# Seven x blocks instead of six, two weight tiles instead of three, and a new order inside a slot of an attention and ffn kernel

## The chip, the cores and the metric

The kernel runs on one core of a Trainium2 chip. The metric is device time in microseconds (us), the median of several runs of the same kernel. The core has five engines that work side by side, each through its own instructions in order: TensorE (PE in the profile, its weight loads PEld), VectorE (DVE), ScalarE (ACT), GpSimd (POOL), and SyncE (SP), which here issues nearly all DMA transfers.

## The reference

```python
def _attn_ref(q, k, v, tau):                      # batch 8, heads 8, sequence 576, head size 64
    scores = matmul(q, k.transpose(0, 1, 3, 2)) / sqrt(64)
    thresh = max(scores, axis=-1) - tau
    scores = where(scores >= thresh, scores, -1e9)
    attn = exp(scores - max(scores, axis=-1))
    attn = attn / (sum(attn, axis=-1) + 1e-09)
    return matmul(attn, v)

def _moe_ref(x, w_a, w_b, w_out):                 # x: 4608 x 512, w_a and w_b: 512 x 1536, w_out: 1536 x 512
    return (x @ w_a) * (x @ w_b) @ w_out
```

All is float32. The output of attention, with its eight heads put side by side, is the x of the second function ("ffn" below).

## The kernel before

**Units and slots.** Attention is cut into 160 units (i, u): i is one of 32 pairs of heads, u one of five query tiles (four of 128 rows, and a tail of 64 rows). The main loop runs over slots g = 0 to 162. Slot g starts unit g and does later steps of earlier units, so that several units are in flight. The order in which instructions are written in a slot is the order in which each engine runs them: `keep_order` fixes it at the end.

**What a slot holds.** From slot 9 on, the order in the program is:

- `scores` (L338): TensorE multiplies q and k of unit g into two PSUM tiles of two banks each (L350); VectorE takes the row maxima (two reductions, L357) and the threshold (L358).
- `turn_blocks` (L439) for unit g−1: VectorE transposes its weights in blocks of 32 (two L444, in place in the tile `tw`), and SP writes them to a scratch tensor in DRAM, `swap`, with four DMAs (L455).
- `advance` with 0.3 of the slot's pace: TensorE does so many columns of ffn work.
- `weigh` (L368) for unit g: ScalarE computes a bias (L377) and the exponential (L378) into a new `tw` tile; VectorE multiplies by the mask of the threshold and sums (L381).
- transposes of freshly loaded q and k (`prep`, L318).
- `advance` with 0.35 of the pace.
- in some slots `weighted` (L531): the product with v of a finished half of a pair (72 matmul records, L481), and the copies out of PSUM into an x block (`settle`, L488 on ScalarE and L490 on VectorE). It is preceded by `make_x`, see below.
- `turn_back` (L458) for unit g−2: SP reads `swap` back into a tile `wT` (one DMA of 576 KB, L464; two of 144 KB for a tail, L467). There are two `wT` tiles, so the DMA waits on SP's queue until the product that read the old content is through.
- `reciprocal` (L392, L394) and `normalise` (two L400 on ScalarE) for unit g.
- loads of q, k and v for later pairs, and stores of finished rows (SP).
- `advance` with 0.15 and 0.2 of the pace.

The first eight units take another way, with transposes on TensorE.

**ffn.** `ffn` (L651) is a generator; each step issues the matmuls of some columns. The products with w_a and w_b are partly plain (L686), partly in a form with seven products in the place of eight (`seven_of`, L587, matmuls in L624), and the product with w_out is L732 (also seven products, L778 for the first two blocks). A seven-product group of 64 matmul records is short, and six of seven groups need VectorE steps (L633 to L647).

**The pacing.** `advance(cols)` adds columns to `running["owed"]` and steps the generator until they are used up. The pace of a slot comes from the backlog and the slots until the next x block arrives; a product with v is deducted.

**x blocks.** Attention's output is gathered in tiles with tag `xT`, of which there are XT_BUFS. A block with the sums for the seven-product form takes four tiles while ffn reads it. `make_x` (L849), called before a product with v that opens a new x tile, counts the tiles in use and, while there are too many, forces ffn on:

```python
        while (len([k for k in x_of if k != (0, 0)]) + len(xtail_of) + len(complete) + sum(len(x) for x, _ in blocks)
               + (state["reading"] and running["tiles"]) + count > XT_BUFS):
            owed = running["owed"]
            running["owed"] = 0.0
            advance(1)
            running["owed"] += owed - 1
            store(len(pending))
```

The forced columns stay in `owed` as debt. A tile for the tails of four batches is in use for most of a half of the run.

**PSUM.** All matmul results go through one pool of four tiles (`banks`, L127), which are used in turn.

Of the kernel before, what the change touches and what calls it, by code (L numbers as in the profile page):

```python
# [21 lines left out]

PV_LAG = 3
BY_PE = 8
XT_BUFS = 6
H_BUFS = 3
Q_BUFS = 3
OSB_BUFS = 5
# [3 lines left out]
ROOM = 1024  # L32
PORTIONS = (0.3, 0.35, 0.15, 0.2)
RAWS = 3
TW_BUFS = 3
SEVENS = 2
BY_HEAD = 16

# [15 lines left out]
def kernel(  # L54
# [38 lines left out]
    nc = tc.nc  # L93
# [11 lines left out]
    R = 96  # L105
# [99 lines left out]
    sums_sb = sums_u32.bitcast(FP32)  # L205
# [71 lines left out]
    ROWS = 2 * NR * D  # L277
    rooms = []
    for _ in range(TW_BUFS):
        t = work.tile([P, 2 * NB, Q], FP32, tag="tw", bufs=TW_BUFS, name="rows")  # L280
        rooms.append(t.rearrange("p n e -> p (n e)")[0:R, 0:ROWS])
    rooms += [sums_sb[0:R, c:c + ROWS] for c in range(0, 5 * ROWS, ROWS)]
    rooms = [t.rearrange("p (n w) -> p n w", n=NR) for t in rooms]
    load_rows(0, "q", rooms[0])
    load_rows(0, "k", rooms[1], nc.scalar)
# [49 lines left out]
    def prep_copy(mT, tp):  # L335
        nc.vector.tensor_copy(mT.rearrange("p (c k) -> p c k", c=2), tp)

    def scores(i, u):  # L338
        qT, kT = prepared[i]["q" if i < HP else "q1" if u > 1 else "q0"], prepared[i]["k"]
        base = HALF if i >= HP and u > 1 else 0  # L340
        n = 2 if u < NT else 1
        sc = [banks(SH, "sc") for _ in range(n)]
        each = [(c, t, j) for c in range(2) for t in range(n) for j in range(2)]
        if units.index((i, u)) < BY_HEAD:
            each.sort(key=lambda x: x[2])
        for c, t, j in each:
            r = slice(j * D, (j + 1) * D)
            o = t if u < NT else 1 - j
            q0, to = (u * P + t * D if u < NT else MAIN) - base, slice(o * D, (o + 1) * D)
            nc.tensor.matmul(sc[j if u < NT else 0][to, c], qT[r, q0:q0 + D],  # L350
                             kT[r, c * SH:(c + 1) * SH], start=True, stop=True)
        mx = small.tile([P, 2], FP32, tag="mx", name="mx")
        thr = small.tile([P, 2], FP32, tag="thr", name="thr")
        bias = small.tile([P, 2], FP32, tag="bias", name="bias")
        for j in range(n):
            c = slice(j, j + 1)
            nc.vector.tensor_reduce(mx[:, c], sc[j], axis=AX.XY, op=ALU.max)  # L357
        nc.vector.tensor_scalar(thr[:, 0:n], mx[:, 0:n], cut, None, op0=ALU.subtract)  # L358
        scored[i, u] = (sc, thr, bias, mx)
# [79 lines left out]
    def turn_blocks(i, u):  # L439

        ws, _ = weights.pop((i, u))
        t = whole.pop((i, u))
        for w in ws:
            nc.vector.transpose(w, w)  # L444
        if u < NT:
            swap = scratch.tile([G, P, NSLOT * Q], FP32, tag="swap", name="swap")
        else:
            swap = scratch.tile([2, P, NSLOT * Q], FP32, tag="swapt", name="swap")
        swaps[i, u] = swap
        for g in range(G):  # L450
            if u < NT:
                to, n = swap[g], G
            else:
                to, n = swap[g % 2, (1 - g // 2) * D:(2 - g // 2) * D], 2
            nc.sync.dma_start(to.rearrange("(r p) e -> p r e", p=Q),  # L455
                              t[g * Q:(g + 1) * Q, 0:n * NSLOT].rearrange("p (r s) e -> p r (s e)", r=n))

    def turn_back(i, u):  # L458

        swap = swaps.pop((i, u)).rearrange("g p e -> p g e")  # L460
        if u < NT or i < HP:
            turned[i, u] = turned_tile()
            n = G if u < NT else 2
            nc.sync.dma_start(turned[i, u][:, 0:n].rearrange("p g s e -> p g (s e)"), swap)  # L464
        else:
            for y in range(2):
                nc.sync.dma_start(turned[i, 2 + y][:, G].rearrange("p s e -> p (s e)"), swap[:, y])  # L467
# [381 lines left out]
    def make_x(count):  # L849

        while (len([k for k in x_of if k != (0, 0)]) + len(xtail_of) + len(complete) + sum(len(x) for x, _ in blocks)
               + (state["reading"] and running["tiles"]) + count > XT_BUFS):
            owed = running["owed"]
            running["owed"] = 0.0
            advance(1)
            running["owed"] += owed - 1
            store(len(pending))

    def backlog():
# [29 lines left out]
    n = 0  # L889
# [4 lines left out]
    for g in range(len(units) + PV_LAG):  # L894
        written = len(pending)
        state["converted"] = state["added"]
        here = g < len(units)
        converting = bool(early.get(g)) or bool(early.get(g - 1))
        if here:
            i, u = units[g]  # L900
            scores(i, u)
        exchange_blocks()
        pace = (PACE if g > BY_PE else PACE_EARLY) * BLOCK_COLS
        if g > BY_PE:
            pace = min(pace, backlog() / (min([a for a in arrivals if a > g] + [len(units) + PV_LAG + 1]) - g))
        pace += NSLOT * S / 2 / (NT + 1) + CATCH_UP * max(backlog() - BLOCK_COLS, 0)
        if 2 <= g < BY_PE + 2:
            weighted_unit(*units[g - 2])
            running["owed"] -= NSLOT * P // 2
        if g < 3:  # L910
            prep_copy(*prep_pe(g + 1, "q"))
        convert_rest(g, 0)
        if g == 0:
            for c in range(0, 3 * QUARTER - 2 * CW + 1, 2 * CW):
                extra.append(more_u32[:, c:c + 2 * CW].rearrange("p (f w) -> p f w", w=2))
        if g == 3:
            for c in range(0, NSUM - 2 * CW + 1, 2 * CW):
                extra.append(sums_u32[:, c:c + 2 * CW].rearrange("p (f w) -> p f w", w=2))
        load_weights(RAWS)
        if g > BY_PE and g <= len(units):  # L920
            turn_blocks(*units[g - 1])
        if g > BY_PE:
            advance(PORTIONS[0] * pace)
        if here:
            weigh(i, u)
        if here and g < BY_PE:
            reciprocal(i, u, nc.vector)
        if 0 < g <= BY_PE:
            turn_pe(*units[g - 1])
        if g < 3:  # L930
            prep_copy(*prep_pe(g + 1, "k"))
        for p in range(HP, NPR):
            for name, d in (("q0", 2), ("k", 1), ("q1", 1)):
                if g == (second if name == "q1" else first)[p] - d:
                    prep(p, name)
        if g > BY_PE:
            advance(PORTIONS[1] * pace)
            n = g - PV_LAG
            if BY_PE <= n < len(units) and part(*units[n]):
                p, h = part(*units[n])  # L940
                if pairs[p][1] == 0:
                    make_x(2 if h == 1 and p >= HP and pairs[p][0] % GT == 0 else 1)
                make_room()
                weighted(*part(*units[n]))
                running["owed"] -= NSLOT * width(*part(*units[n])) // 2
            if BY_PE + 1 < g <= len(units) + 1:
                turn_back(*units[g - 2])
        for n in early.get(g, [])[:1]:
            convert_first(n)
            convert_clamp(n)  # L950
        if here and g < BY_PE:
            diagonals(i, u)
        elif here:
            reciprocal(i, u, nc.scalar if converting else nc.vector)
            normalise(i, u)
        convert_rest(g, 1)
        if g <= BY_PE:
            advance(pace)
        convert_rest(g, 2)
        for n in early.get(g, [])[1:]:  # L960
            convert_first(n)
            convert_clamp(n)
        load_weights(RAWS)
        for p in range(HP, NPR):
            for name, d in (("q0", 4), ("k", 3), ("q1", 3)):
                if g == (second if name == "q1" else first)[p] - d:
                    load(p, name)
        for p in range(1, NPR):
            if g == first[p] - 1:
                load_v(p)  # L970
        if BY_PE <= g < BY_PE + HP:
            load_v(g - BY_PE, again=True)
        store(written)
        if g > BY_PE:
            advance(PORTIONS[2] * pace)
            advance(PORTIONS[3] * pace)

        if not converting and not state["sums"]:
            state["slots"] = state.get("slots", 0) + 1
            for n in {1: (0,), 2: (1,), 3: (2,)}.get(state["slots"], ()):  # L980
                for z in range(2):
                    weight_sums(n, z)
            if state["slots"] >= 3 and state["through"]:
                for z in range(2):
                    weight_sums(3, z)
                state["sums"] = True
        if g > first[HP] + 1 and not converting and state["first"] < 3 * SEVENS:
            first_sums(state["first"] % 3, state["first"] // 3)
            state["first"] += 1
# [37 lines left out]
```

## Time and profile before

| what | value |
| --- | --- |
| median of 3 runs | 1502.7 us (1501.66 to 1507.4) |
| time of the profiled run | 1505.54 us |
| span of the profiled run, first to last instruction | 1503.7 us |
| mean granted TensorE clock | 0.984 |
| TensorE busy | 1401.6 us (93%) |
| VectorE busy | 1069.6 us (71%) |
| ScalarE busy | 687.7 us (46%) |
| GpSimd busy | 553.3 us (37%) |
| one L444 transpose, mean | 754 ns |
| one L357 maximum, mean | 749 ns |
| one L378 exponential, mean | 831 ns |
| one L381 thresholding, mean | 801 ns |
| one L400 normalisation, mean | 769 ns |

The page of a profile gives busy time per engine, the same in 40 slices of time with the granted TensorE clock, the DMA queues, the chain of work that ended last, and groups of instructions. In a group, "out<-in" names the tiles, then come the shapes, the count, the busy time, the mean of one, and the idle time of the engine just before them with what ended it. Other views answer questions on the same trace: waits (who waited for whom, total us, times, longest), stretches of time with each engine's busy time, and a timeline. The profiled run is the one whose span and durations are used; the median is of separate runs. Slot numbers are counted by the L350 matmuls, 16 records for a unit of 128 rows and 8 for a tail.

### The profile page before, as it was taken

The page shows a single profiled execution, that of the slowest core. Times are in us where ns is not written, and L with a number is a line of the kernel's source. Part 1 is how long each engine was busy: PE and PEld are TensorE (multiplying, and loading weights), DVE is VectorE, ACT ScalarE, POOL GpSimd, SP SyncE. Part 2 cuts the span into 40 slices and gives each one's busy share as a digit, 9 for nine tenths or more (in the row PEclk, how much of TensorE's full clock was granted, in tenths as well). Part 3 has the DMA queues.
Part 4 walks back from the last instruction along what each step waited for, and adds up shares of the span by engine and source line. Part 5 has one row for each costly group of instructions (what it writes and reads, how often), then busy time and mean ns, then how long its engine had stood idle before and what let it go on. Part 6 is the DMA issues. An engine that isn't in the chain of part 4 may idle for free.

```text
span 1503.7 us, 76562 instructions
## 1 busy us (share of the span) xinstructions
PE 1401.6 (93%) x34208; PEld 1231.2 (82%) x34208; DVE 1069.6 (71%) x2365; ACT 687.7 (46%) x1275; POOL 553.3 (37%) x724
## 2 busy tenths in 40 slices
PE   5789999999899999999997979899999999999998
PEld 4677687788899888889796878888789877888986
DVE  6798687888767786777647767667867877764434
ACT  5777355545454554544424435345444545431111
POOL 2664704433252525252623225251525161614100
PEclk9999999999999999999997999999999999999999
DMA  9976687668656775676526756367655776550000
GB/s 214 214 205 179 164 191 179 164 154 214 155 151 159 186 181 146 157 183 165 131 58 159 169 140 166 91 160 182 167 152 132 180 174 166 135 147 29 4 17 17
DMA packets 325081, 223.22 MB, mean 148 GB/s; under 512 B 169616, under 2 KB 308880, under 8 KB 324752
## 3 DMA queue, kind: packets, MB, share of 16 engines
q1 hardware_dynamic: 322384, 217.73, 59.0%
q8 instruction: 269, 4.41, 1.3%
q10 hardware_dynamic: 2368, 0.59, 0.2%
q14 instruction: 60, 0.49, 0.1%
HBM read 128.58 MB, written 89.65 MB: 145 GB/s over the span
## 4 chain that ended last, share of the span: by engine, by line
PE 77%; DVE 11%; DMA 4%; issue 3%; ACT 2%; SPq 2%; DVEq 0%; ACTq 0%
PE pab L624 20%; PE po L732 19%; PE pab L686 17%; PE pv L481 9%; PE sc L350 9%; DVE mx L357 3%; DMA wT<-swap 2%; DVE tw L444 2%; SPq L455 1%; DVE tw L381 1%; PE po L778 1%; DVE xT L490 1%; PE tp L425 1%; DVE low L258 0%; DMA qT<-in_q_dram 0%
## 5 line engine op out<-in xcount | busy, mean ns | idle before, releaser
L400 ACT ACTIVATE tw<-tw,rcp 128x576 f32<-128x576 f32 x272 | 197.8, 769 | 218.3 <-DVE rcp L394 218.3
L357 DVE TENSOR_REDUCE mx<-sc 128x1 f32<-128x576 f32 x288 | 205.2, 749 | 93.6 <-PE sc L350 86.1
L378 ACT ACTIVATE tw<-sc,bias,scalars 128x576 f32<-128x576 f32 x288 | 239.3, 831 | 9.8 <-ACT bias L377 0.2
L381 DVE SCALAR_TENSOR_TENSOR tw<-sc,thr,tw 128x576 f32<-128x576 f32 x288 | 224.0, 801 | 9.8 <-ACT tw L378 8.6
L732 PE MATMUL po<-wo_sb,h 64*64 64x256 f32 x3264 | 223.0, 380 | 4.0 <-DVE t L642 1.9
L350 PE MATMUL sc<-kT,qT 64*64 64x288 f32 x2016 | 192.9, 412 | 15.7 <-issue 7.4
L590 POOL TENSOR_TENSOR t<-u,t 128x512 f32<-128x512 f32 x28 | 35.6, 1273 | 457.5 <-ACT t L631 355.2
L444 DVE STREAM_TRANSPOSE tw<-tw 128x576 f32<-128x576 f32 x272 | 196.1, 754 | 0.8 <-ACT tw L400 0.8
L481 PE MATMUL pv<-wT,vm 64*64 64x160 f32 (+3 forms) x5184 | 182.6, 275 | 11.9 <-DMA wT<-swap 10.4
L701 POOL TENSOR_TENSOR h<-h 128x256 f32<-128x256 f32 x168 | 117.4, 730 | 202.0 <-PE po L732 198.5
L732 PEld LDWEIGHTS po<-wo_sb,h 64*64 64x64 f32 x3264 | 165.4, 134 | 29.9 <-DVE t L642 2.4
L481 PEld LDWEIGHTS pv<-wT,vm 64*64 64x64 f32 x5184 | 165.0, 134 | 22.3 <-issue 11.4
L732 PE MATMUL po<-sums_u,h 64*64 64x256 f32 x2448 | 161.8, 381 | 0.0
L350 PEld LDWEIGHTS sc<-kT,qT 64*64 64x64 f32 x2016 | 111.9, 136 | 44.2 <-issue 20.4
L624 PE MATMUL pab<-xU,wb_sb 64*64 64x128 f32 x4096 | 139.2, 270 | 2.4 <-issue 2.2
L732 PEld LDWEIGHTS po<-sums_u,h 64*64 64x64 f32 x2448 | 123.0, 135 | 20.2
L624 PEld LDWEIGHTS pab<-xU,wb_sb 64*64 64x64 f32 x4096 | 126.2, 133 | 5.4 <-issue 3.4
L490 DVE COPY xT<-pv 64x128 f32<-64x128 f32 (+1 forms) x136 | 38.1, 280 | 126.3 <-ACT xT L488 125.1
L377 ACT ACTIVATE bias<-mx,scalars 128x1 f32<-128x1 f32 x288 | 82.9, 288 | 74.9 <-DVE mx L357 74.4
L631 ACT COPY t<-pab 128x512 f32<-128x512 f32 x96 | 55.6, 581 | 124.1 <-PE pab L624 122.8
L488 ACT COPY xT<-pv 128x128 f32<-128x128 f32 (+1 forms) x68 | 17.7, 260 | 197.4 <-PE pv L481 197.4
L624 PE MATMUL pab<-xS,wa_sb 64*64 64x128 f32 x2048 | 104.3, 270 | 1.6 <-issue 1.5
(135 smaller groups left out, 2583.7 us busy)
## 6 DMA issues: line engine op xcount, KB each, us to landing
swap<-tw SPq DMA_DIRECT2D x480, 144.0 KB, 2.6
wT<-swap SPq DMA_DIRECT2D x120, 576.0 KB, 4.7
vm<-in_v_dram SPq DMA_DIRECT2D x128, 72.0 KB, 3.2
swap<-tw SPq DMA_DIRECT2D x128, 72.0 KB, 1.8
kT<-in_k_dram SPq DMA_DIRECT2D x112, 72.0 KB, 4.4
wT<-swap SPq DMA_DIRECT2D x56, 144.0 KB, 3.1
out_dram<-kept SPq DMA_DIRECT2D x30, 256.0 KB, 4.1
qT<-in_q_dram SPq DMA_DIRECT2D x112, 40.0 KB, 4.4
```

What stands on the lines that cost most here:

```text
L350: nc.tensor.matmul(sc[j if u < NT else 0][to, c], qT[r, q0:q0 + D], kT[r, c * SH:(c + 1) * SH], start=True, stop=True)
L357: nc.vector.tensor_reduce(mx[:, c], sc[j], axis=AX.XY, op=ALU.max)
L377: nc.scalar.activation(bias[:, j:j + 1], mx[:, j:j + 1], AF.Copy, scale=e_nscale)
L378: nc.scalar.activation(wb[j], sb[j], AF.Exp, bias=bias[:, j:j + 1], scale=e_scale)
L381: nc.vector.scalar_tensor_tensor(out=wv, in0=sb[j], scalar=thr[:, j:j + 1], in1=wv, op0=ALU.is_ge, op1=ALU.mult, accum_out=sums[:, j:j + 1])
L400: nc.scalar.activation(w, w, AF.Copy, scale=rcp[:, j:j + 1])
L444: nc.vector.transpose(w, w)
L481: nc.tensor.matmul(pv[c * D:(c + 1) * D, y], vm[rows, s], wT[y](rows, s), start=(s == 0), stop=(s == NSLOT - 1))
L624: nc.tensor.matmul(pab[c * D:(c + 1) * D, r, y * P:(y + 1) * P], w[k][rows, w0:w0 + D], moving[k][rows], start=(k == 0), stop=(k == HP - 1))
L686: nc.tensor.matmul(pab[c * D:(c + 1) * D, r], w[rows, f // n, k, fs + c * D:fs + (c + 1) * D], moving, start=(k == 0), stop=(k == H - 1))
L701: (nc.vector if state["over"] else nc.gpsimd).tensor_tensor(*a, **kw)
L732: nc.tensor.matmul(po[c * D:(c + 1) * D, r, y], ht[rows, t0:t0 + D], other[rows, f], start=(f == 0), stop=(f == NF // 2 - 1))
```

## The change

- `XT_BUFS` becomes 7 and `TW_BUFS` 2. A block of x is 4 KB in each partition, a weight tile 4.6 KB. Of the eight rooms that hold the first rows of q and k, two instead of three are now weight tiles, and six lie in `sums_sb`.
- In `make_x` the forced columns are no longer left in `owed`.
- `turn_blocks` of unit g−1 is called inside `scores`, after the matmuls and ahead of the maxima; its DMA issues come with it, ahead of `exchange_blocks`, the early weight loads, and all else of the slot.
- `reciprocal` and `normalise` of unit g come right after the second `advance`, ahead of `make_x`, the product with v and `turn_back`. (Slot 8 keeps the old place.)
- `turn_back` issues one DMA for each of the four parts of a unit of 128 rows, and two for a tail of the first pairs.

```diff
-XT_BUFS = 6
+XT_BUFS = 7
-TW_BUFS = 3
+TW_BUFS = 2
...
-    rooms += [sums_sb[0:R, c:c + ROWS] for c in range(0, 5 * ROWS, ROWS)]
+    rooms += [sums_sb[0:R, c:c + ROWS] for c in range(0, 6 * ROWS, ROWS)]
...
-    def scores(i, u):
+    def scores(i, u, meanwhile):
...
+        meanwhile()
         mx = small.tile([P, 2], FP32, tag="mx", name="mx")
...
             n = G if u < NT else 2
-            nc.sync.dma_start(turned[i, u][:, 0:n].rearrange("p g s e -> p g (s e)"), swap)
+            for y in range(n):
+                nc.sync.dma_start(turned[i, u][:, y].rearrange("p s e -> p (s e)"), swap[:, y])
...
             advance(1)
-            running["owed"] += owed - 1
+            running["owed"] = owed
             store(len(pending))
...
+        def turn():
+            if g > BY_PE and g <= len(units):
+                turn_blocks(*units[g - 1])
+
         if here:
             i, u = units[g]
-            scores(i, u)
+            scores(i, u, turn)
+        else:
+            turn()
         exchange_blocks()
...
         load_weights(RAWS)
-        if g > BY_PE and g <= len(units):
-            turn_blocks(*units[g - 1])
...
             advance(PORTIONS[1] * pace)
+            if here:
+                reciprocal(i, u, nc.scalar if converting else nc.vector)
+                normalise(i, u)
             n = g - PV_LAG
...
-        elif here:
+        elif here and g == BY_PE:
             reciprocal(i, u, nc.scalar if converting else nc.vector)
             normalise(i, u)
```

## The prediction

> **What bounds the kernel now.** I read the page's engine rows first, then the chain, then a table of stretches, and last the waits.
>
> ```profile
> PE 1401.6 (93%) x34208; PEld 1231.2 (82%) x34208; DVE 1069.6 (71%) x2365; ACT 687.7 (46%) x1275; POOL 553.3 (37%) x724
> ...
> PEclk9999999999999999999997999999999999999999
> ...
> PE 77%; DVE 11%; DMA 4%; issue 3%; ACT 2%; SPq 2%; DVEq 0%; ACTq 0%
> ```
>
> TensorE is the bound: it is busy 93% and carries 77% of the chain. Its 102 us of idle time are the most that reordering can return, plus what a reduced clock costs (the 9 and 7 in the clock row). So the question is where these 102 us lie. Pricing matmuls needs a stretch without waits, and the chain's end has one, after the attention work:
>
> ```profile
> 1383.62 13.71 PE pab L686 x255
> 1397.33 24.45 PE pab L624 x893
> ...
> 1421.88 18.13 PE po L732 x334
> ```
>
> That is 53.8 ns for an L686 matmul, 27.4 for L624, 54.3 for L732. Sixteen score matmuls start within about 1.1 us (70 ns each), and a product with v (72 matmuls) takes about 2.3 us. With these I priced the matmuls of every slot from 20 to 158 and subtracted the sum from the slot's length. Three kinds come out. 81 slots with little L624 work lose 4.7 us in all, 0.06 each: TensorE runs without a break. 48 slots with over 100 L624 matmuls lose 36 us, 0.75 each. Ten slots, in three places, lose 33 us. The table of stretches shows the first place slot by slot (slots 93 to 96), with an ordinary slot (52) and an L624 slot (87) after it; columns are stretch, length, then busy time (and instructions) of PE, weight loads, DVE, ACT, POOL, then clock and DMA:
>
> ```profile
> 760.00:788.80 28.80, 28.80 (x990) 28.41 (x989) 12.33 (x20) 4.54 (x8) 7.63 (x6) 1.00 0.11 25
> 788.80:791.10 2.30, 1.54 (x32) 1.01 (x23) 1.03 (x5) 0.45 (x2) 0.00 (x0) 1.00 0.23 38
> 791.10:796.40 5.30, 2.57 (x16) 1.32 (x18) 4.31 (x12) 3.62 (x7) 0.00 (x0) 0.69 0.52 154
> 796.40:809.50 13.10, 7.07 (x84) 5.68 (x83) 8.27 (x18) 5.21 (x9) 0.00 (x0) 0.50 0.67 170
> ...
> 423.10:430.80 7.70, 7.70 (x145) 7.02 (x139) 6.31 (x13) 3.98 (x9) 7.21 (x13) 1.00 0.68 156
> ...
> 704.30:714.80 10.50, 9.14 (x307) 8.67 (x300) 7.28 (x18) 5.87 (x10) 3.83 (x3) 1.00 0.64 169
> ```
>
> Slot 93 is a flood: `make_x` has no x block free and drives 712 forced matmuls of ffn. The columns are then charged as debt, so the next three slots get no ffn work and show attention's bare latency, and the clock falls to 0.50. Slots 104–106 and 113–115 are the same. TensorE's timeline names what ends the gaps:
>
> ```profile
> 791.14 0.67 PE L350 MATMUL sc<-kT,qT 64*64 64x288 f32 x2 [0.80 <-DVE xt L490]
> 794.50 4.11 PE L350 MATMUL sc<-kT,qT 64*64 64x288 f32 x22 [2.69 <-DVE tw L381]
> 804.64 5.29 PE L481 MATMUL pv<-wT,vm 64*64 64x160 f32 x70 [6.03 <-DMA wT<-swap]
> ```
>
> For the reordering, the waits of VectorE and SP matter:
>
> ```profile
> DVE mx L357 <- PE sc L350: 86.1, 64, 4.7
> ...
> SPq L455 <- DVE tw L444: 319.4, 112, 8.2
> SPq L464 <- PE pv L481: 138.9, 46, 23.3
> ```
>
> **What the Trainium skill says.** "TensorE: Matmul & The Clock Gate", What's actually happening: the array runs at half clock after an idle window of about 3.4 us. The trace agrees: 0.50 in the stretch after the 2.69 us gap. "Perfetto Trace Analysis", Optimization Strategy: a repeated bubble can mean too few buffers for the next tile; here it is the x blocks. The same page, Identifying Dependency Chains: waits on several engines may become extra semaphore instructions; the trace shows such ones ahead of L481, 51 ns each. "DMA: Bandwidth & Descriptors", Rules for kernel authors, advises joining small transfers; the change splits one of 576 KB into four of 144 KB, and the trace prices both below.
>
> **The change part by part.**
>
> *Seven x blocks.* I stepped the kernel's own counters (owed columns, backlog, x blocks in use) through all 163 slots. With six blocks this gives the L624 counts of slots 93, 104 and 113 (880, 472, 448; the trace has 880, 472, 449). With seven, `make_x` never has to force anything. Slots 93 to 96 then get 216, 296, 280 and 88 L624 matmuls; the blocks, their seven-product form and the ending (1792 L624 matmuls after slot 162) stay as they are, so TensorE's work is the same to the matmul. The gain: the three places last 49.5 + 36.1 + 32.3 = 117.9 us; their work is 1801 × 27.4 ns + 264 × 54.3 ns + 136 × 70 ns + 5 × 2.3 us = 84.7 us. Some 33 us are lost, including the half clock. In their stead come about nine more L624 slots, at 0.75 us each: 7 us. Net **−26 us**. Late next in these slots is VectorE, as in every L624 slot.
>
> *Not charged later.* This line runs only inside `make_x`'s loop, which is never entered with seven blocks: 0.
>
> *Transposes first.* Per slot two L444 transposes (1.43 us as a pair), with the swap writes they release, go ahead of the two maxima (1.4 us); the sum on VectorE is unchanged. Where VectorE waits for the scores (64 waits, 86.1 us, 1.35 us each) they fill that wait, and the thresholding L381 comes up to 1.4 us earlier. Where it doesn't wait, the maxima start 1.4 us later, and the exponentials (two of 0.29 + 0.83 us on ACT) that the transposes covered are bare: 0.6 us later for the second L381. Who waits for L381 is TensorE, for the scores' PSUM. From an L381's end to the next use of its PSUM tile the records have a median of 1.8 us when scores come next and 1.1 us for an L624 group (12 of 63 under 0.3). So a delay of 0.6 us is hidden in ordinary slots and costs some tenths in the others. The bounds: every such L624 wait goes, −12 us; or all 48 slots take the 0.6 us in half, +15 us. I take **+2**, since gain and loss fall on different slots.
>
> *Normalisation ahead of the product with v.* The reciprocal and two L400 (1.44 us) no longer stand behind the copies out of the product, so the transposes that now open the next slot find their input ready; behind them are those copies on ACT and DVE, late by up to 0.3 us on DVE and 1.5 on ACT when VectorE is behind. 0, since product tiles are reused only four allocations later.
>
> *Two weight tiles.* The exponential of unit g then waits for the swap writes of unit g−2 instead of g−3. Today those land 1.7 us (median) before it; 30 of 136 units would be late, by 31 us in all. The writes now go out after transposes that end near 2 us into a slot rather than 4.7 us, so most of the 30 disappear; those where SP itself is late (29 units start their writes over 0.5 us after the transposes) stay. ACT would stall some 15 us, with everything queued behind the exponential, of which TensorE sees a part: **+4** (0 to 15).
>
> *Reads in four parts.* 120 reads become 480 and four become eight: 364 more issues.
>
> ```profile
> L464 SPq DMA_DIRECT2D wT<-swap x124: 376/382/1812, 109.9 to 1349.0; - x124
> ...
> wT<-swap SPq DMA_DIRECT2D x120, 576.0 KB, 4.7
> ```
>
> At 0.43 us with the gap, SP gets 157 us more, about 1.3 per read. Its two waits above (458 us over 152 units, 3 us each) cover it on average; queued behind are loads, stores and the next swap writes. In slots with loads of q, k and v it doesn't fit so easily: 22 issues per two slots become 28, at 0.5 us 14 of 15.6 us. The last part is issued 1.3 us after the first, and a write of 144 KB lands in 2.6 us: 3.9 against 4.7, so the product's input is rather earlier. Outside the floods TensorE waits 4.4 us for it: **−2**. Each product now waits on up to eight transfers instead of two to four, one to two more semaphore instructions of 51 ns, 53 times: **+4** (0 to 8).
>
> *The early rooms* change at the start only, and six rooms of 768 columns are exactly the 4608 there: 0.
>
> Sum: −26 + 2 + 0 + 4 − 2 + 4 = −18 us. The span of 1503.7 us (profiled run 1505.5) becomes 1485.7. The median, 1502.7 us, lies 1.0 below the span; I take **1485**.
>
> **Rivals.**
> (a) *Floods gone, L624 slots gain too:* the earlier L381 removes a third or more of their 36 us: 1485 − 12 = 1473. For: TensorE's waits in these slots name L381 and the VectorE steps behind it. Against: VectorE is nearly full there.
> (b) *The gain is mostly eaten:* SP saturates in the load-heavy slots (8 of 20), and exponentials and products wait for landings: four such two-slot steps per batch group at 0.6 us over seven groups, +17: 1502. For: 28 issues in 15.6 us.
> (c) *Slower: attention's chain becomes the bound of ordinary slots.* In the new order it is serial: transposes 1.4, first maximum 0.7, two exponentials 2.3, second L381 0.8, reciprocal 0.4, first L400 0.8, hops 0.3 = 6.7 us, plus an evacuation (0.67) and a q or k transpose (0.44 to 0.77) between them: 7.8–8.1, against ordinary slots of 7.0–7.8. Today a slot's maxima don't wait for the last slot's transposes. It decides from 0.14 us per slot over 129 slots (18 us); at 0.35 us it is +45: 1530. Against: the slack of 1.8 us in PSUM, and evacuations that fill the gaps.
>
> **How the numbers follow.** The sum's case 0.52 (1476 to 1496), (a) 0.14, (b) 0.16, (c) 0.18. Below 1465 or above 1516 I leave 0.2. About 0.5% (7.5 us) is what a measurement can tell from no change: faster (under 1495.2) takes (a) and most of the sum's case, 0.63; same 0.18; slower 0.19.
>
> **What would show it.** No slot over 13 us, no stretch at clock 0.5 after slot 10, and slots 93–96 near 38 us: seven blocks right. L357's wait for L350 well under 86 us, and L381 not later against the slot: the order right. Slots like 52 at 8 us or more with TensorE waiting on L381: (c). L378 or L481 waiting on DMA in load-heavy slots: (b).

## The result, and the profile after

The changed kernel takes 1505.6 us (median, 1496.4 to 1510.5), the kernel before in the same comparison 1503.7 us. The ratio is 1.0003, with a 95% interval from 0.9987 to 1.0020: no difference that can be measured. The forecast was 1485 us. The profiled run has a span of 1505.3 us.

The floods are gone all the same. The page after, its engine row, its clock row and its chain by engine:

```profile
PE 1409.5 (94%) x34208; PEld 1249.6 (83%) x34208; DVE 1082.3 (72%) x2365; ACT 689.8 (46%) x1275; POOL 554.2 (37%) x724
...
PEclk9899999999999999999999999999999999999999
...
PE 62%; DVE 15%; SPq 7%; ACT 6%; DMA 5%; issue 5%; POOL 0%; DVEq 0%; ACTq 0%; POOLq 0%
```

The clock row no longer shows the dip of the second half. But a digit stands for 37.6 us, and short falls don't show in it. Five of them are left from slot 10 on, two of these in the second half (columns: stretch, length, then busy time (and instructions) of PE, weight loads, DVE, ACT, POOL, then clock and DMA):

```profile
859.03:862.45 3.42, 3.42 (x59) 3.23 (x54) 3.08 (x6) 1.77 (x4) 0.00 (x0) 0.50 0.81 180
1026.29:1029.70 3.41, 3.31 (x64) 3.31 (x68) 3.19 (x7) 0.71 (x2) 2.48 (x2) 0.50 0.73 164
```

Together they last 17.1 us, where the falls before, all in the flood places, lasted 30.7 us. At half clock 17.1 us cost at most half of it, 8.5 us (an estimate). TensorE carries only 62% of the chain instead of 77%; VectorE, SP and ScalarE carry more. The stretches of slots 93 to 96 after, then slot 52 (the same columns):

```profile
780.10:789.30 9.20, 9.20 (x299) 8.85 (x295) 4.81 (x11) 2.87 (x5) 1.28 (x1) 1.00 0.31 68
789.30:800.40 11.10, 9.87 (x325) 9.15 (x320) 9.67 (x21) 4.75 (x10) 2.55 (x2) 1.00 0.58 151
800.40:809.50 9.10, 8.81 (x304) 8.55 (x299) 5.83 (x13) 5.12 (x9) 3.43 (x3) 1.00 0.39 104
809.50:817.70 8.20, 8.20 (x223) 7.91 (x219) 6.14 (x13) 1.91 (x3) 0.40 (x1) 1.00 0.31 76
436.70:444.40 7.70, 7.70 (x145) 7.70 (x138) 5.93 (x11) 4.03 (x8) 7.19 (x13) 1.00 0.75 174
```

The four slots last 37.6 us instead of 49.5, all at full clock. I priced the slots again as in the prediction, and subtracted the work from the length. The ten flood slots lose 4.6 us instead of 32.9; slots with over 100 L624 matmuls as much as before (36.4, was 35.9). The slots that lost next to nothing before, 4.7 us in 81 of them, now lose 33.0 us in 82. That is where the gain went. Slot 52 is not among them. The losses lie in the slots of units with u = 0 or 1, and nearly all of them in those with u = 1. In most of these, v is loaded and k is transposed for later pairs; a product with v is issued in none of them. The waits after name the engines:

```profile
DVE tw L382 <- ACT tw L379: 54.9, 119, 3.1
...
DVE tw L445 <- ACT tw L401: 30.6, 42, 0.8
...
DVE mx L358 <- PE sc L350: 17.7, 15, 3.1
...
ACT tw L379 <- DMA swap<-tw: 14.7, 13, 3.4
```

(L358 is the maximum, L379 the exponential, L382 the thresholding, L401 the normalisation, L445 the transpose; before they were L357, L378, L381, L400 and L444.) Two of these waits in the kernel before:

```profile
DVE tw L381 <- ACT tw L378: 8.6, 23, 1.2
...
DVE tw L444 <- ACT tw L400: 0.8, 1, 0.8
```

VectorE's wait for the scores fell from 86.1 to 17.7 us, as the reordering was to bring about. In its place it waits for the exponentials, 54.9 us instead of 8.6, and for the normalisation, 30.6 instead of 0.8: 68 us less of one wait, 76 more of two others.

### The profile page after: what moved, and what is told of

It is laid out like the page before. It is cut to its first block, busy times and chain, and to the rows that moved or that the text cites. A ratio compares the mean times of both kernels' runs of the same rounds, so it can differ in the third digit from the quotient of the medians.

```text
span 1505.3 us, 76983 instructions
## 1 busy us (share of the span) xinstructions
PE 1409.5 (94%) x34208; PEld 1249.6 (83%) x34208; DVE 1082.3 (72%) x2365; ACT 689.8 (46%) x1275; POOL 554.2 (37%) x724
## 4 chain that ended last, share of the span: by engine, by line
PE 62%; DVE 15%; SPq 7%; ACT 6%; DMA 5%; issue 5%; POOL 0%; DVEq 0%; ACTq 0%; POOLq 0%
PE po L734 16%; PE pab L626 16%; PE pab L688 15%; PE pv L483 7%; PE sc L350 7%; DVE tw L445 3%; DVE tw L382 3%; SPq L456 2%; DVE mx L358 2%; ACT tw L379 2%; DMA swap<-tw 2%; SPq L148 2%; SPq L466 2%; ACT tw L401 2%; DMA qT<-in_q_dram 1%
## 5 line engine op out<-in xcount | busy, mean ns | idle before, releaser
L401 ACT ACTIVATE tw<-tw,rcp 128x576 f32<-128x576 f32 x272 | 198.2, 771 | 244.9 <-DVE rcp L395 244.7
L382 DVE SCALAR_TENSOR_TENSOR tw<-sc,thr,tw 128x576 f32<-128x576 f32 x288 | 232.9, 816 | 77.8 <-ACT tw L379 54.9
L379 ACT ACTIVATE tw<-sc,bias,scalars 128x576 f32<-128x576 f32 x288 | 239.7, 832 | 24.4 <-DMA swap<-tw 14.7
L734 PE MATMUL po<-wo_sb,h 64*64 64x256 f32 x3264 | 219.0, 380 | 5.8 <-DVE kept L473 4.1
L445 DVE STREAM_TRANSPOSE tw<-tw 128x576 f32<-128x576 f32 x272 | 197.5, 760 | 32.6 <-ACT tw L401 30.6
L358 DVE TENSOR_REDUCE mx<-sc 128x1 f32<-128x576 f32 x288 | 201.0, 733 | 17.8 <-PE sc L350 17.7
L378 ACT ACTIVATE bias<-mx,scalars 128x1 f32<-128x1 f32 x288 | 83.7, 291 | 236.8 <-DVE mx L358 236.8
L688 PE MATMUL pab<-xS,wa_sb 64*64 64x256 f32 (+1 forms) x1536 | 106.2, 366 | 0.0
L688 PE MATMUL pab<-xT,wa_sb 64*64 64x256 f32 (+1 forms) x1408 | 94.4, 362 | 6.8 <-DVE xT L492 1.9
```

The lines of the kernel that those rows point to most:

```text
L378: nc.scalar.activation(bias[:, j:j + 1], mx[:, j:j + 1], AF.Copy, scale=e_nscale)
L379: nc.scalar.activation(wb[j], sb[j], AF.Exp, bias=bias[:, j:j + 1], scale=e_scale)
L382: nc.vector.scalar_tensor_tensor(out=wv, in0=sb[j], scalar=thr[:, j:j + 1], in1=wv, op0=ALU.is_ge, op1=ALU.mult, accum_out=sums[:, j:j + 1])
L401: nc.scalar.activation(w, w, AF.Copy, scale=rcp[:, j:j + 1])
L688: nc.tensor.matmul(pab[c * D:(c + 1) * D, r], w[rows, f // n, k, fs + c * D:fs + (c + 1) * D], moving, start=(k == 0), stop=(k == H - 1))
L734: nc.tensor.matmul(po[c * D:(c + 1) * D, r, y], ht[rows, t0:t0 + D], other[rows, f], start=(f == 0), stop=(f == NF // 2 - 1))
```

## The experiments

In all of them the ratio is to the kernel before, with its 95% interval. A difference between two ratios is turned into microseconds at 15 us for 1%; with the intervals it is good to some 5 us. Waits and timelines come from one profiled run of each kernel. That of the first kernel is the fastest of its six runs (1469.4 us at a mean granted clock of 0.999; the medians are 1479.0 and 0.994), so a difference to it that rests on traces alone can be some microseconds too large.

**What ate the gain: the reads, the order, or the tiles?** Four kernels. The first has seven blocks and two tiles alone:

```diff
-XT_BUFS = 6
+XT_BUFS = 7
-TW_BUFS = 3
+TW_BUFS = 2
...
-    rooms += [sums_sb[0:R, c:c + ROWS] for c in range(0, 5 * ROWS, ROWS)]
+    rooms += [sums_sb[0:R, c:c + ROWS] for c in range(0, 6 * ROWS, ROWS)]
```

> The kernel before with seven x blocks and two weight tiles, and nothing else of the change. SP theory (the reads in four parts fill SP's queue in the slots that also load q, k and v, so that swap writes go out late and the exponential, with two tiles only, waits for them): the floods' 28 us go and two tiles alone cost 4 to 8, so about 1480 us. Order theory (transposes first makes attention's chain longer in the slots with loads and uses up the gain): also about 1480. Tiles theory (two tiles cost it, whatever the order and the reads): 1497 to 1504.

Measured: 1479.0 us, 0.9833 (0.9797 to 0.9869). So blocks and tiles alone have the whole gain that was forecast for the change, and two tiles are not what eats it. The clock is a small part of the 26 us between it and the change: the median granted clock of the runs is 0.994 here and 0.990 there, worth some 6 us at most (an estimate: 0.4% of the time). Below, "the first kernel" is this one.

The second is the changed kernel with single reads (and the old line in `make_x`, which with seven blocks changes nothing):

```diff
-            for y in range(n):
-                nc.sync.dma_start(turned[i, u][:, y].rearrange("p s e -> p (s e)"), swap[:, y])
+            nc.sync.dma_start(turned[i, u][:, 0:n].rearrange("p g s e -> p g (s e)"), swap)
```

> The changed kernel with each product's input read back by one DMA again. SP theory: most of the 28 us that came back in ordinary slots is gone, about 1480 us. Order theory and tiles theory: it stays, 1498 to 1506.

Measured: 1502.4 us, 1.0000 (0.9979 to 1.0022). The SP theory, which I held, fell: without the reads in four parts nothing comes back. The new order alone takes 25 us from blocks and tiles.

The third has the old order and keeps the reads in four parts (the first kernel with the read loop of the change):

> The changed kernel with transposes and normalisation at their old places, seven blocks, two tiles and reads in four parts kept. SP theory: SP is as full as in the changed kernel and the swap writes go out still later in the slot, so no gain over the changed kernel: 1503 to 1515 us. Order theory: about 1480. Tiles theory: 1500 or more.

Measured: 1490.6 us, 0.9917 (0.9891 to 0.9943). It beats the changed kernel, against the SP theory, but is no 1480 either: here the reads cost 12.6 us. The fourth puts the read loop alone into the kernel before:

> The kernel before with the reads in four parts alone; three tiles and six blocks stay. SP theory: SP is late in the same slots, but three tiles leave a median 9.7 us between a write's landing and the exponential that needs the tile, so only products that wait for their input lose: 1503 to 1512 us. Order theory and tiles theory: as the kernel before, 1502 to 1505.

Measured: 1514.6 us, 1.0081 (1.0050 to 1.0113): again 12 us, a little above the range that I gave. With three tiles no exponential waits for a swap write in this kernel's trace; what grows is TensorE's wait for the product's input (10 waits, 15.2 us, against 5 and 10.4 before) and the time at half clock (44.3 us from slot 10 on, against 30.7). So with the old order the reads cost 12 us, with the new one 0.5. Both parts cost, and not as a sum.

**The two halves of the order, and the tiles.** The next kernel is the first one with the transposes first, and the normalisation left at its old place:

```diff
+        meanwhile()
         mx = small.tile([P, 2], FP32, tag="mx", name="mx")
...
-            scores(i, u)
+            scores(i, u, turn)
...
-        if g > BY_PE and g <= len(units):
-            turn_blocks(*units[g - 1])
```

> Seven blocks, two tiles, single reads, and the transposes first in a slot; the normalisation stays behind the product with v. Against seven blocks and two tiles alone (1479 us) the full reordering cost 23 us. Normalisation theory (ScalarE waits at the normalisation for the reciprocal, and the copies out of the product and of the ffn's output groups, which TensorE needs for PSUM, now stand behind it): this kernel has none of that, 1476 to 1486 us. Transposes theory (exponentials without cover delay the thresholding and all behind it on VectorE): 1495 to 1505.

Measured: 1525.7 us, 1.0140 (1.0115 to 1.0164). Transposes first cost 46 us by themselves, nearly twice the 25 that both halves cost together. The other half alone, the first kernel with the normalisation ahead:

```diff
             advance(PORTIONS[1] * pace)
+            if here:
+                reciprocal(i, u, nc.scalar if converting else nc.vector)
+                normalise(i, u)
             n = g - PV_LAG
...
-        elif here:
+        elif here and g == BY_PE:
```

> Seven blocks, two tiles, single reads, and the normalisation ahead of the product with v; the transposes stay at their old place in the middle of the slot. Normalisation theory: it carries most of the 23 us, 1493 to 1503 us, and ScalarE's copies of po stand behind the normalisation and its wait for the reciprocal. Transposes theory: 1476 to 1486.

Measured: 1493.3 us, 0.9921 (0.9899 to 0.9943): 13 us. Neither theory had both sizes right. And two tiles alone in the kernel before, `TW_BUFS` 2 with the six rooms:

> The kernel before with two weight tiles alone; the floods stay. The prediction's term for it was +4 (0 to 15): 1504 to 1512 us. If it costs nothing, 1500 to 1504; then the blocks alone give the 23 us that blocks and tiles gave together.

Measured: 1509.1 us, 1.0045 (1.0028 to 1.0061): 6.8 us. From this kernel to the first one only the blocks change, from 1.0045 to 0.9833: seven blocks bring 32 us.

*Why transposes first cost.* VectorE's waits in the first kernel (seven blocks and two tiles, old order):

```profile
DVE mx L357 <- PE sc L350: 79.7, 69, 3.7
...
DVE tw L381 <- ACT tw L378: 22.8, 50, 2.7
```

and in the kernel with the transposes first:

```profile
DVE tw L445 <- ACT tw L401: 81.9, 103, 0.8
DVE tw L382 <- ACT tw L379: 51.7, 118, 2.4
...
DVE mx L358 <- PE sc L350: 15.5, 18, 2.3
```

The wait for the scores is filled, 64 us less. But at its head VectorE now meets a normalisation that has only just been issued (81.9 us, in 103 slots), and with the maxima done there is nothing left to do beside the first exponential (29 us more). These three changes add up to 46 us, the size of the loss. (Other waits of VectorE moved as well, by up to 9 us each, so this is a fit and not a proof; the run with the transposes between the maxima, below, is the test.) In the slots of u = 0 and 1 the first maximum begins 3.6 us into the slot instead of 1.8, and the second thresholding ends 7.6 us into it instead of 6.9 (means; the medians are 3.70 and 1.61, 7.70 and 6.82). With the normalisation ahead as well, as in the change, 51 of the 82 us of the first wait go, which fits that both halves together cost less than the first alone.

*Why the normalisation ahead costs.* Slot 127 shows it. The timeline in the first kernel (columns: start, duration, engine, line, operation, tiles, count, and in brackets the idle time before and what ended it):

```profile
1041.93 0.58 ACT L470 COPY kept<-po 128x512 f32<-128x512 f32 x1
...
1043.75 0.27 ACT L488 COPY xT<-pv 128x128 f32<-128x128 f32 x1 [1.25 <-PE pv L481]
...
1045.34 1.44 ACT L400 ACTIVATE tw<-tw,rcp 128x576 f32<-128x576 f32 x2 [1.32 <-DVE rcp L394]
```

and in the changed kernel with single reads:

```profile
1068.30 1.44 ACT L401 ACTIVATE tw<-tw,rcp 128x576 f32<-128x576 f32 x2 [1.82 <-DVE rcp L395]
...
1069.64 0.56 ACT L471 COPY kept<-po 128x512 f32<-128x512 f32 x1
1070.11 0.26 ACT L489 COPY xT<-pv 128x128 f32<-128x128 f32 x1
...
1070.24 0.69 DVE L472 TENSOR_TENSOR kept<-kept,po 128x512 f32<-128x512 f32 x1 [1.97 <-ACT kept L471]
...
1071.08 0.66 PE L733 MATMUL po<-wo_sb,h 64*64 64x256 f32 x8 [2.39 <-DVE kept L472]
```

Before, ScalarE copied ffn's group of `po` out of PSUM right after the exponentials, and came to the normalisation last. Now it stands 1.82 us at the normalisation, waiting for the reciprocal, works 1.44 us on it, and the copy that has been ready all the while comes behind. VectorE's second half of that copy waits 1.97 us for it, and TensorE 2.39 us for the PSUM tile. The slot in the first kernel and in this one:

```profile
1043.40:1050.50 7.10, 7.10 (x138) 6.83 (x131) 6.95 (x18) 4.00 (x8) 6.79 (x11) 1.00 0.69 178
...
1066.60:1078.80 12.20, 9.54 (x142) 7.00 (x138) 8.93 (x21) 5.47 (x11) 8.53 (x13) 0.86 0.58 144
```

Not all of the 5.1 us is the normalisation's: this kernel has the transposes first as well, and the clock fell to half for 3.4 us of the slot. With the normalisation ahead alone the slot takes 9.3 us at full clock. That kernel has the same wait of TensorE in the same slot, 1.80 us, and in slot 29, 1.91. Over its whole run TensorE waits 3.7 us for ffn's `po` to be copied and 5.9 us, in four places, for another copy on ScalarE (`h`, L692); in the first kernel these are none and 0.5. That is 9 of the 13 us; the rest is not traced to a line.

**Is the transposes' loss a matter of what stands beside the exponentials?** The first kernel with the transposes between the two maxima:

```diff
             nc.vector.tensor_reduce(mx[:, c], sc[j], axis=AX.XY, op=ALU.max)
+            if j == 0:
+                meanwhile()
```

> Seven blocks, two tiles, single reads, normalisation at its old place, and the transposes between the first and the second maximum of a slot. Cover theory (transposes first costs because the first exponential has no VectorE work beside it and because VectorE opens the slot with a wait for the normalisation): the first exponential is covered again and the first maximum fills the wait, so most of the 46 us between 0.983 and 1.014 is back, 0.984 to 0.996. If any delay of a maximum costs the same, 1.005 to 1.015.

Measured: 1482.6 us, 0.9892 (0.9864 to 0.9919): 37 of the 46 us are back. One maximum of about 0.73 us ahead of the transposes decides; they then wait 9.9 us for the normalisation instead of 81.9, and thresholding 15.8 us for the exponentials instead of 51.7.

**Where do the reads in four parts cost?** SP's queue in the changed kernel around slot 41, with ScalarE's exponentials, from the timeline:

```profile
340.34 3.51 SPq L148 DMA_DIRECT2D kT<-in_k_dram  x4
...
343.89 2.01 SPq L171 DMA_DIRECT2D vm<-in_v_dram  x4
346.00 1.81 SPq L456 DMA_DIRECT2D swap<-tw  x4
347.90 3.24 SPq L466 DMA_DIRECT2D wT<-swap  x4
...
350.71 0.83 ACT L379 ACTIVATE tw<-sc,bias,scalars 128x576 f32<-128x576 f32 x1 [1.47 <-DMA swap<-tw]
```

The transposes of the unit written here ended at 341.6 us, but SP was busy with loads until 345.9, issued the swap writes 4.4 us late, and the exponential that takes the tile over waited for the last to land. In the first kernel 25 units start their swap writes over 0.5 us after their transposes, in the third 57, in the changed one 82. To relieve SP, the third kernel (old order, reads in four parts) got the loads of q, k and v on GpSimd's queue:

```diff
-                    load(p, name)
+                    load(p, name, nc.gpsimd)
...
-                    nc.sync.dma_start(half[c * Q:(c + 1) * Q], rows[:, c])
+                    (nc.sync if again else nc.gpsimd).dma_start(half[c * Q:(c + 1) * Q], rows[:, c])
```

> Seven blocks, two tiles, old order, reads in four parts (1490.6 us as it was), with the loads of q, k and v for the pairs after the first four issued from GpSimd's queue instead of SP's. SP theory: what the reads in four parts cost (12 us) is their place in SP's queue among these loads, so it goes: 1477 to 1484 us. Other theory (the cost is in TensorE's extra semaphores or in DMA traffic, not in SP): 1488 to 1494.

Measured: 1491.3 us, 0.9914 (0.9885 to 0.9943), no gain. But the waits did move. Only 3 units still start their swap writes late, ScalarE's wait for landings of swap writes is 9.6 us instead of 35.9 in the third kernel, and SP stands ahead of the transposes again:

```profile
SPq L455 <- DVE tw L444: 422.9, 143, 8.1
```

against 169.4 us, 77 times, in the third kernel and 331.7 with single reads. So a control was needed, the same loads on GpSimd's queue with single reads:

> Control for the run with reads in four parts and loads moved (0.9914 of the kernel before): seven blocks, two tiles, old order, single reads, with the loads of q, k and v issued from GpSimd's queue. That run's trace has new waits of 1.3 to 2.6 us for GpSimd's xS sums. If the moved loads cost something by themselves, and the reads in four parts nothing once SP is relieved (SP theory), this is equal to it: 0.989 to 0.994. If the reads in four parts cost their 12 us whatever SP does, this is 0.981 to 0.985.

Measured: 1492.9 us, 0.9942 (0.9921 to 0.9964). The moved loads cost 1.1% by themselves; TensorE and its weight loads wait 17.5 us for GpSimd's tile `xS` there (7.9 in the first kernel). On top of them the reads in four parts cost nothing that can be measured. This points to their place in SP's queue for the 12 us, rather than to TensorE's extra semaphores or the transfers themselves, which the kernel with the moved loads has as well. It is not a proof, since the moved loads could cover the reads' cost, as the new order does. The Trainium skill, "DMA: Bandwidth & Descriptors", Issuing engines are not separate DMA queues, says that issuing from several engines only saves issue time, usually small beside the transfer. Here one issue is shorter than its transfer too (four reads were issued in 3.24 us above, and one takes 2.9 us to landing). But issues add up: the sixteen above keep SP busy from 340.3 to 351.1 us, and what the next step waits for stands behind them.

**Is one part enough to blame in the full change?** The changed kernel with the transposes between the maxima, by the same edit:

> The changed kernel, all of it, but with the transposes between the first and the second maximum instead of ahead of both. Cover theory: the transposes' place is the main part of what ate the gain. What stays are the normalisation ahead (13 us alone), two tiles (7 us) and the reads in four parts (up to 12 us): 0.984 to 0.994 of the kernel before. If the normalisation and the reads alone are enough to eat it, once both are there, 0.997 to 1.003.

Measured: 1495.8 us, 0.9960 (0.9939 to 0.9981), between the two ranges; the interval reaches into both. And the changed kernel with the transposes at their old place, behind both maxima (the first kernel with the normalisation ahead and the read loop):

> The changed kernel with the transposes at their old place behind both maxima: seven blocks, two tiles, normalisation ahead, reads in four parts. The parts' costs alone are 0.88% (normalisation) and 0.84% (reads) on top of 0.983. If they add: 0.998 to 1.002, and the transposes' place costs nothing more once both are there. If the normalisation's wait covers the late reads as the transposes' place does (costs overlap): 0.990 to 0.995.

Measured: 1497.5 us, 0.9975 (0.9958 to 0.9992): the costs of normalisation and reads nearly add, 21 us of 26. So in the full change the transposes' place costs only 4 us more, and the reads 0.5: neither is the sole cause. The change without the normalisation ahead was not run. They meet in the same slots. There are 38 slots of u = 0 and 1 with no more than 100 L624 matmuls. What they lose (length less priced work) and how long VectorE is idle in them, from the profiled executions:

| kernel | ratio | loss, us | VectorE idle, us |
| --- | --- | --- | --- |
| before | 1 | 6.8 | 51.6 |
| seven blocks, two tiles | 0.9833 | 8.0 | 53.7 |
| and transposes between the maxima | 0.9892 | 9.9 | 55.2 |
| and normalisation ahead | 0.9921 | 17.7 | 63.4 |
| and reads in four parts | 0.9917 | 24.2 | 69.6 |
| and normalisation ahead, reads | 0.9975 | 23.1 | 71.7 |
| and transposes first | 1.0140 | 27.7 | 73.4 |
| and transposes first, normalisation ahead | 1.0000 | 26.4 | 70.3 |
| the change | 1.0003 | 27.5 | 72.2 |

The loss is VectorE's idle time less 44 to 49 us in every row. This alone doesn't make VectorE the cause: the work in these slots is nearly the same in all rows, so when they get longer, every engine is idle for longer by as much. ScalarE's idle time less the loss is as steady, 138 to 144 us in the eight kernels with seven blocks. The table shows where the time goes; which wait takes it must be read from the chain of work that ended last. Within these slots VectorE and ScalarE carry 13 us of it in the first kernel, 103 with the transposes first, and 67 in the change; SP carries 16, none and 37. With the reads in four parts alone VectorE and ScalarE stay at 14 and SP rises to 32. So the parts lengthen different links, and what fits the table is that they do not add because one wait covers another. That the loss stops at 23 to 28 us is an observation; I did not show what stops it. Transposes first alone lose another 30 us in the L624 slots (60.8 against 31.2), where the other kernels show 28 to 42 without a pattern.

**A version that beats both.** Seven blocks with three tiles, old order and single reads. Room comes from smaller pools, and from a matrix that is put into free columns:

```diff
-XT_BUFS = 6
-Q_BUFS = 3
-OSB_BUFS = 5
+XT_BUFS = 7
+Q_BUFS = 2
+OSB_BUFS = 4
...
-    ident = const.tile([P, P], FP32, name="ident")
+    ident = sums_sb[:, 4096:4096 + P]
```

> Seven blocks with three weight tiles, old order, single reads. To make room, four ffn output tiles instead of five, two q tiles instead of three, and the identity matrix lies in columns of the sums that are free at the start. If two tiles cost the 0.45% measured with six blocks and the smaller pools cost nothing: 0.977 to 0.981. If the smaller pools bring waits of their own: 0.983 or more.

Measured: 1469.4 us, 0.9796 (0.9768 to 0.9824), 2% faster than both kernels. The interval overlaps that of two tiles (0.9833), so that the third tile helps here too is likely and not shown. In the 38 slots it loses 1.2 us.

## Why the prediction was wrong

**Seven x blocks, −26: right.** Measured 32, by the ratios 1.0045 and 0.9833, with an error of some 6 us; the flood slots lose 28 us less in the trace, and slots 93 to 96 last 37.6 us against the 38 forecast. From slot 10 to slot 158 none is longer than 11.9 us. The clock was read too simply, though. Its falls between slot 10 and the ending last 3.4, 6.8 or 17.1 us, whole multiples of 3.41, which fits the window of about 3.4 us that the prediction names. But the gap that it points to is shorter, 2.69 us, and the clock fell 1.3 us into it, at 793.1. And without floods it can still fall: five times in the change, while the first kernel's profiled run has no fall from slot 10 to the ending.

**Not charged later, 0; the rooms, 0: not tested on the chip.** With seven blocks the program with the old line is the same, instruction for instruction on every engine.

**Two weight tiles, +4: right within its bounds.** Measured 6.8 (4 to 9), but with the old order. In the change ScalarE waits 14.7 us for swap writes, as the "some 15" said.

**Transposes first, +2 (−12 to +15): wrong, the first step that failed.** Its picture was that the transposes fill the wait for the scores and that a delay of 0.6 us in the thresholding is hidden. The first half came true. But the bounds counted the delay only in the L624 slots, trusting a median of 1.8 us of slack in PSUM elsewhere, and they left out the wait at VectorE's head: a transpose that opens the slot waits for a normalisation that closed the last one. It waits 81.9 us for it with the transposes first alone, and 30.6 in the change. Alone the step costs 46 us; both halves of the order, forecast at +2, cost 25.

**Normalisation ahead, 0: wrong, the second.** It named the copies that now stand behind, "late by up to 0.3 us on DVE and 1.5 on ACT", and dismissed them by the four allocations until a product tile is reused. It took the delay on ScalarE to be the duration of the normalisation. ScalarE also waits for the reciprocal there, 1.82 us in slot 127, and what is behind is not only the product's copy but ffn's `po`, whose tile TensorE needs within the slot. Alone 13 us. It also is what makes transposes first bearable: of the 46 us it takes 21 off.

**Reads in four parts, −2 and +4: wrong with the old order, near in the change by luck.** The issue cost of 0.43 us was right for most, but that SP's waits "cover it on average" averaged over slots of two kinds. The prediction saw 14 of 15.6 us taken in the load-heavy ones and put no cost on it. With the old order the reads cost 12 us, very likely there; in the change the new order's waits hide them.

**The sum.** Measured parts, each step on top of the last: +7 for the tiles, −32 for the blocks, +25 for both halves of the order, +0.5 for the reads behind it: +0.5. They add up because they are steps of one path; alone, the three parts cost 46, 13 and 12 us. The prediction had −26 + 4 + 2 + 2 = −18, so the new order is what it missed.

**The rivals.** (a) did not come: the L624 slots lose as much as before. (b) had the size (1502), by luck, and a true mechanism, SP in load-heavy slots, but it was not what held the changed kernel there. (c) had the chain right, and its price for a bad case, 1530 us, is near the 1525.7 of transposes first alone, by luck again. It had the wrong place: slots like 52 keep their 7.7 us; those that lose are mostly the ones with k to prepare. A view that could have warned was VectorE's idle time by kind of slot, 51.6 us in 38 slots or 1.4 us in each, not its 71% over the span. Of the signs named, two came out wrong: "no stretch at clock 0.5 after slot 10", and "L381 not later against the slot" (in the slots of u = 0 and 1 its second one ends 7.4 us into the slot on average, 6.6 before). L357's shorter wait came true and did not show the order to be right.

## What to carry to other kernels

An instruction that is moved forward on an in-order engine takes its wait along, and everything behind it pays wait and duration both; list all that stands behind, of other streams too, and ask who needs it soonest. A filled wait is a gain only if the chain after it doesn't stretch by as much: work that stood beside an exponential is cover, and taking it away shows in the next wait of the same engine. Run the parts of a bundle one by one, since here one part worth 32 us was hidden by four others, each of which cost time alone. And idle time of an engine that grows as fast as a stretch does is no sign of a cause: every engine's does.

## What the runs showed of the hardware that was not expected

Issues on SP's queue are not alike: issuing four loads of k took 3.51 us around slot 41, one of them 1.54, while four of v took 2.01 and four swap writes 1.81. And moving the q, k and v loads to GpSimd's queue cost 1.1%, although it relieved SP. And the clock fell to half without a long gap: in the kernel before at 793.1 us, 1.3 us into a gap of 2.69 us, with TensorE busy for 1.3 of the 3.4 us ahead of the fall.
